# Small matmuls of a linear-attention kernel issued as 32x32 blocks instead of block-diagonal pairs

## The chip, the cores and the metric

The kernel runs on one core of a Trainium2 chip. The core has a matrix engine (PE, with its weight loads shown as PEld), a vector engine (DVE), a scalar engine (ACT), a general-purpose engine (POOL) and a queue engine for transfers (SP), which run in parallel and wait for each other through semaphores (in the kernel before, PE, DVE, ACT and POOL are busy for 244.6, 187.9, 184.3 and 169.9 of 289.8 us, and POOL waits 46.9 us for ACT at line 914). The metric is the device time in microseconds, lower is better; medians of several executions are quoted. Profiled executions show a span, from the first to the last instruction, that is about 1.7 us shorter than the time measured for the same execution. PE's clock is granted at full or at half rate in the clock records of the two traces, which begin at 60.9 us before and 72.5 us after the change. Ahead of that the starts of the matmuls show it: the 128-column transposes of the kernel before (line 643) start 107 ns apart before 60 us and 56 ns apart at 147 to 235 us (medians). "Warm" means the full rate.

## The reference, cut to what matters

```python
# attention: 4 batches, 8 heads, 768 steps, head size 48
k_n = k / (norm(k) + 1e-6)
state = 0                                   # (4, 8, 48, 48)
for t in range(768):
    y[:, :, t] = g[:, :, t] * (q[:, :, t] @ state)
    v_old = state^T k_n[:, :, t]
    state = state + beta[:, :, t] * outer(k_n[:, :, t], v[:, :, t] - v_old)
# then an MLP over 3072 tokens: 384 -> 2048 -> 384
h = x @ w_in
g = where(h >= 1, h, where(h <= -1, 0, (h + 1)**2 / 4))
return g @ w_out
```

The loop over 768 time steps is rewritten in 24 steps of 32. Inside a step the sequential update becomes a 32x32 triangular system for each of 32 pairs of batch and head. The Gram matrix k k^T gives the system, a recursion on 16x16 halves and two merge products invert it, and a masked score matrix k q^T gives the output inside the step.

## The kernel before: the parts that matter

The kernel is a list of tasks. A search in Python decides, before anything runs, the order of the tasks on each engine; then the instructions are emitted in that order. Partitions 0 to 127 hold four batches of 32 rows each. The products below are done for two batches at once, with 64x64 matrices of which only the two diagonal 32x32 blocks are wanted.

```python
# Grams and scores of one step (the unsplit form): 64 rows of stationary, 128 columns moving
for j in range(4 * hf, 4 * hf + 4):
    for G in range(2):                        # two pairs of batches
        r = slice(64 * G, 64 * G + D)
        nc.tensor.matmul(b[64 * G:64 * G + 64, 128 * jj:128 * jj + 128], kt[r, j, 0, :],
                         kt[r, j].rearrange("p a t -> p (a t)"), ...)
# DVE: mask off everything but the lower triangles of the diagonal blocks, twice per step
nc.vector.tensor_tensor(out=amt[:, 4 * hf:4 * hf + 4, 0:128], in0=bank, in1=mask, op=mult)
...
# inverse: DVE transposes 32x32 blocks of the masked Grams, both halves are added, the recursion follows
nc.vector.transpose(out=at, in_=am)           # 128 x 1024
...
# merge products: 32 matrices, block-diagonal stationary
for m in range(32):
    for G in range(2):
        r = slice(64 * G, 64 * G + 64)
        nc.tensor.matmul(b[r, 16 * m:16 * m + 16], am[r, slot + m // J, m % J, 0:64], d0[r, m, 0:16], ...)
...
# masked scores
for j in range(J):
    for G in range(2):
        r = slice(64 * G, 64 * G + 64)
        nc.tensor.matmul(b[r, D * j:D * j + D], amt[r, j, 64:128], u16[r, j, :], ...)
```

Each matmul is two PE instructions in the trace (6,091 LDWEIGHTS and 6,091 MATMUL records in the kernel before): one loads one operand, the stationary matrix, and one streams the other, the moving matrix, through.

Of the kernel before, what the change touches and what calls it, by code (L numbers as in the profile page):

```python
# [33 lines left out]
LAT = 0.12  # L34
# [22 lines left out]
class Task:  # L57
    __slots__ = ("opts", "reads", "writes", "deps", "pred", "succ", "left", "ready", "start", "end", "d", "eng", "fn", "kind", "name", "n",
                 "cost", "nmm", "mode", "gate", "psum", "held", "seq", "lag", "after")
# [35 lines left out]
class Plan:  # L95
# [3 lines left out]
    def add(self, eng, dur, fn, reads=(), writes=(), kind="", name="", alt=(), nmm=0, mode=None, seq=None, prio=0.0):  # L99
        t = Task([(eng, dur, fn)] + list(alt), list(reads), list(writes), kind, name)  # L100
        t.nmm, t.mode, t.n, t.seq = nmm, mode, len(self.tasks), seq
        self.tasks.append(t)
        for v in t.reads:
            v.r.append(t)
        for v in t.writes:
            v.w.append(t)
        return t
# [57 lines left out]
    def forward(self, A):  # L165
        T = self.tasks
        free = dict.fromkeys(ENGS, 0.0)
# [7 lines left out]
        big = []  # L175
# [14 lines left out]
        while left:  # L190
# [48 lines left out]
            if e == "PE":  # L239
                gap = s - free["PE"]  # L240
                if WARM0 < s < WARM1 and gap > 0.6:
                    n = min(int((gap - 0.3) / 0.11 * WSHARE), 24)
                    w = free["PE"] + 0.05
                    warm.append((w, n))
                    big.append((w, w + 0.055 * n))
                    mode = "F"
                while big and big[0][1] < s - 3.4:
                    big.pop(0)
                if sum(y - max(x, s - 3.4) for x, y in big) < 0.8:
                    d *= 1.8  # L250
                if mode is not None and t.mode != mode:
                    d += 0.1
                mode = t.mode
                d = fetch.take(2 * t.nmm, s, d, True)
                if t.mode == "F":
                    big.append((s, s + d))
# [29 lines left out]
            for u in t.succ:  # L286
                u.left -= 1
                r = (t.end if t in u.deps else t.start) + (LAT if e != u.opts[0][0] else 0.0) + u.lag
                if r > u.ready:
                    u.ready = r  # L290
                if not u.left:
                    for o in u.opts:
                        cand[o[0]].append(u)
        self.span = max(t.end for t in T)
        self.warms = warm
        return sorted(order, key=lambda t: (t.start, t.n))

    def backward(self):
# [11 lines left out]
        while n:  # L310
# [14 lines left out]
            for u in t.pred:  # L325
                left[u] -= 1
                r = end + (LAT if e != u.eng else 0.0) + t.lag if u in t.deps else s
# [7 lines left out]
    def plan(self, passes):  # L335
        import random
        rnd = random.Random(7)
        A, best, bestA, stale, hist = self.first(), None, None, 0, []
        for i in range(passes):
            order = self.forward(A)  # L340
            if order is None:
                stale = 9
                hist.append("x")
            else:
                hist.append(round(self.span, 1))
                B = self.backward()
                if best is None or self.span < best[0] - 1e-6:
                    best = (self.span, order, [(t, t.start, t.end, t.eng, [v.bank for v in t.psum]) for t in order], self.warms)
                    bestA, stale = B, 0
                    self.bestA = A  # L350
                else:
                    stale += 1
                A = B
            if stale >= 3:
                A = [x + rnd.gauss(0.0, NOISE) for x in (bestA or A)]
        if PRINT:
            print(hist)
        self.span = best[0]
        for t, t.start, t.end, t.eng, banks in best[2]:
            for v, b in zip(t.psum, banks):  # L360
# [13 lines left out]
def kernel(  # L374
# [42 lines left out]
    mask = tl("mask", [2, 2, 32], FP)  # L417
# [3 lines left out]
    par = tl("par", [2], FP)  # L421
# [14 lines left out]
    AW = 130  # L436
# [3 lines left out]
    R_at = ring("at", 1, [32, 32, 2])  # L440
# [7 lines left out]
    R_p16 = ring("p16", 1, [32, 2, 32])  # L448
# [34 lines left out]
    def load_task(tile_, src, names, cost, val, eng="SP", dur=0.46, kind="load"):  # L483
        def fn(tile_=tile_, src=src):
            ENG[eng].dma_start(out=tile_, in_=src)  # L485
        def fp(tile_=tile_, src=src):
            nc.gpsimd.dma_start(out=tile_, in_=src)  # L487
        t = P.add(eng, dur, fn, [], [val], kind, names, seq="ld",
                  alt=[("POOL", 0.6, fp)] if names[2] in FLEX and int(names[3:]) > 1 else [])
# [51 lines left out]
    vc, vid, vpar = Val("mask"), Val("ident"), Val("par")  # L541
# [6 lines left out]
    def c_mask():  # L548
        nc.gpsimd.memset(ones[:], 1.0)
        nc.gpsimd.memset(mask[:], 0.0)  # L550
        for h4 in range(4):
            r = slice(32 * h4, 32 * h4 + 32)
            nc.gpsimd.affine_select(out=mask[r, :, h4 % 2, :], in_=ones[r, :].rearrange("p (a t) -> p a t", a=2), compare_op=ALU.is_gt, fill=0.0,
                                    base=0, pattern=[[0, 2], [1, 32]], channel_multiplier=-1)

    def c_par():
        nc.gpsimd.memset(par[:], 0.0)
        for h4 in range(4):
            nc.gpsimd.memset(par[32 * h4:32 * h4 + 32, h4 % 2:h4 % 2 + 1], 1.0)
# [5 lines left out]
    P.add("POOL", 1.0, c_ident, [], [vid], "", "ident")  # L565
    P.add("POOL", 1.5, c_mask, [], [vc], "", "mask")
# [8 lines left out]
    P.add("POOL", 0.5, c_par, [], [vpar], "", "par")  # L575
    vtab = Val("tab")
    P.add("DVE", 0.08, lambda: nc.vector.memset(tab[:], 1.0), [], [vtab], "", "tab0")
    P.add("ACT", 1.4, lambda: act("ACT", tab[:], tab[:], AF.Sqrt), [vtab], [Val("tab2")], "", "tab")
# [3 lines left out]
    P.add("POOL", 1.2, lambda: nc.gpsimd.memset(R_p16.tiles[0][:], 0.0), [], [vzp], "", "zp16", alt=[("DVE", 0.91, lambda: nc.vector.memset(R_p16.tiles[0][:], 0.0))])  # L582
# [4 lines left out]
    def prep_pair(p):  # L587
# [5 lines left out]
        P.add("ACT", acost(768), lambda: act("ACT", sqt[:], flat(kt_), AF.Square), [kv], [sq], "", f"ksq{p}",  # L593
# [6 lines left out]
        P.add("DVE", 0.2, lambda: nc.vector.reciprocal(out=nt[:, 3], in_=nt[:, 2]), [v2, nv], [v3], "", f"rcp{p}")  # L600
# [54 lines left out]
    def gram(s):  # L655
        gi = s // GS
        kv, kt = vkt[s]
        vq = vqt[s]
        av, amt = R_am.new(f"am{s}")
        mv = R_mm.new(f"mm{s}")[0]  # L660
        vam[s] = (av, amt, [mv])
        if SPLIT[gi]:
            for v_, a_ in ((av, 0), (mv, 1)):
                gp = pv("c", f"gp{s}_{a_}")

                def fn(gp=gp, a_=a_):
                    b = bk(gp)
                    for j in range(J):
                        for G in range(2):
                            r = slice(64 * G, 64 * G + D)  # L670
                            nc.tensor.matmul(b[64 * G:64 * G + 64, 64 * j:64 * j + 64], kt[r, j, 0, :], kt[r, j, a_, :], start=(j == 0), stop=True, skip_group_check=True)  # L671
                P.add("PE", pe_dur(16, 20), fn, [kv] + (vq if a_ else []), [gp], "fill", f"{'gh'[a_]}r{s}", nmm=16, mode="Q", seq="hr" if a_ else "gr")
                if a_ == 0 and gi < NSPLIT:
                    for sl in range(2):
                        P.add("ACT", acost(256), lambda gp=gp, sl=sl: act("ACT", amt[:, :, 32 * sl:32 * sl + 32], _ap(bk(gp), [[64, J], [1, 32]], 32 * sl), scale=par[:, sl:sl + 1]),
                              [gp, vpar], [v_], "", f"m{s}_{a_}")
                    continue
                P.add("DVE", dcost(512), lambda gp=gp, a_=a_: nc.vector.tensor_tensor(  # L678
                    out=amt[:, :, 64 * a_:64 * a_ + 64], in0=bk(gp)[:].rearrange("p (j x) -> p j x", j=J),
                    in1=_ap(mask, [[0, J], [1, 64]], 64 * a_), op=ALU.mult), [gp, vc], [v_], "", f"m{s}_{a_}")  # L680
            return
        for hf in range(2):
            gp = pv("c", f"gp{s}_{hf}")

            def fn(gp=gp, hf=hf):
                b = bk(gp)
                for j in range(4 * hf, 4 * hf + 4):
                    for G in range(2):
                        r = slice(64 * G, 64 * G + D)
                        jj = j - 4 * hf  # L690
                        nc.tensor.matmul(b[64 * G:64 * G + 64, 128 * jj:128 * jj + 128], kt[r, j, 0, :], kt[r, j].rearrange("p a t -> p (a t)"),
                                         start=(jj == 0), stop=True, skip_group_check=True)
            P.add("PE", pe_dur(8, NS_GR), fn, [kv] + vq, [gp], "fill", f"gr{s}_{hf}", nmm=8, mode="Q", seq="gr")
            P.add("DVE", dcost(512), lambda gp=gp, hf=hf: nc.vector.tensor_tensor(
                out=amt[:, 4 * hf:4 * hf + 4, 0:128], in0=bk(gp)[:].rearrange("p (j x) -> p j x", j=4),
                in1=_ap(mask, [[0, 4], [1, 128]]), op=ALU.mult), [gp, vc], [av, mv], "", f"m{s}_{hf}")

    def inverse(gi):
# [4 lines left out]
        def op(n, kind, reads, writes, name, **aps):  # L703
            def make(e):
                return (e, dcost(n) if e == "DVE" else pcost(n) + (0.12 if name[0] == "s" else 0.0),
# [4 lines left out]
        P.add("DVE", dcost(1024), lambda: nc.vector.transpose(out=at[:].bitcast(FP).rearrange("p a t w -> p (a t w)"), in_=_wap(am, [[1, 32], [AW // 2, 32]], slot * J * AW // 2)),  # L710
              avs, [tv], "", f"at{gi}")
        xv, x = R_x.new()
        for blk in range(2):
            o = 8 * blk * 64 + 32 * blk
            op(256, ALU.add, [tv], [xv], f"prea{gi}", out=_ap(x, [[32, 8], [16, 2], [1, 16]], 256 * blk),
# [334 lines left out]
```

## Time and profile before

| | before |
|---|---|
| time, median (lowest to highest) | 291.06 us (289.87 to 291.66), 3 runs |
| PE instructions (weights and matmuls) | 12,184 |
| first state product (line 834) / first MLP matmul (line 906) | 42.9 / 54.3 us |
| last PE matmul starts | 282.7 us |
| busy: PE, DVE, ACT, POOL | 244.6, 187.9, 184.3, 169.9 us of 289.8 |

The page and the timeline of this profile are read in the prediction below, with its lines. The timeline gives start, duration, engine, source line, operation and, in brackets, the idle time before it with what ended it. "x14" means fourteen such instructions in a row, and "issue" means that the engine waited for nothing that the profile shows.

### The profile page before, as it was taken

To read this page: it belongs to the slowest core of one execution; us is meant where nothing else is said; L and a number is where in the kernel's file an instruction comes from. 1 tells how busy PE (TensorE), PEld (TensorE's weight loads), DVE (VectorE), ACT (ScalarE), POOL (GpSimd) and SP (SyncE) were. 2 spreads that over 40 slices of the span, in tenths; PEclk is the share of its full clock that TensorE was granted. 3 is DMA by queue.
4 is the path that set the end of the run, shared out by engine and by line. 5 is a ranking of instruction groups with operands and counts; after the bars stand their busy time and mean duration, and the time that the engine had idled before them with its cause. 6 is when DMAs were issued, how large, how long until landed. Compare 5 with 4: busy or idle time off the path is not lost.

```text
span 289.8 us, 13941 instructions
## 1 busy us (share of the span) xinstructions
PE 244.6 (84%) x6091; PEld 161.6 (56%) x6091; DVE 187.9 (65%) x348; ACT 184.3 (64%) x325; POOL 169.9 (59%) x309
## 2 busy tenths in 40 slices
PE   0266497895979989996799999999999999999990
PEld 0254486674856665653556565665657555555560
DVE  3699996864875546895687787767954375456200
ACT  1664344377456878965888587887683686797410
POOL 7693059592768794798873598841882272354000
PEclk9999999999587999999699999999999999999997
DMA  6689575989398575277421267532421110111121
GB/s 107 106 173 167 91 141 92 219 129 184 50 208 149 101 123 136 56 152 161 101 41 43 60 128 154 105 81 50 88 56 33 32 32 3 31 32 33 49 79 53
DMA packets 88525, 27.74 MB, mean 96 GB/s; under 512 B 80320, under 2 KB 86976, under 8 KB 88464
## 3 DMA queue, kind: packets, MB, share of 16 engines
q1 hardware_dynamic: 77456, 18.35, 32.7%
q0 software_dynamic: 6752, 7.72, 14.3%
q10 hardware_dynamic: 4256, 0.79, 1.5%
q8 instruction: 47, 0.77, 1.1%
q14 instruction: 14, 0.11, 0.1%
HBM read 25.26 MB, written 4.72 MB: 103 GB/s over the span
## 4 chain that ended last, share of the span: by engine, by line
PE 60%; DVE 13%; DMA 8%; issue 6%; POOL 5%; ACT 3%; SPq 3%; ACTq 0%; DVEq 0%; POOLq 0%
PE bank L933 19%; PE bank L906 18%; DMA rk<-in_k_dram 6%; POOL rk L487 3%; DVE xx L706 3%; PE bank L769 3%; SPq L485 3%; PE bank L671 2%; PE sps L846 2%; PE bank L860 2%; PE bank L834 2%; PE bank L643 2%; DVE tm L706 2%; DMA rv<-in_v_dram 2%; PE bank L876 2%
## 5 line engine op out<-in xcount | busy, mean ns | idle before, releaser
L906 PE MATMUL bank<-xt,win 128*128 128x512 f16 (+1 forms) x336 | 79.1, 369 | 2.2 <-issue 1.4
L917 DVE SCALAR_TENSOR_TENSOR gt<-bank,r 128x512 f16<-128x512 f32 x96 | 64.1, 682 | 24.2 <-ACT r L471 12.7
L933 PE MATMUL bank<-wout,gt 128*128 128x384 f16 x384 | 72.6, 327 | 0.0
L471 ACT ACTIVATE rl<-bank 128x512 f32<-128x512 f32 x96 | 56.4, 597 | 17.3 <-PE bank L906 15.4
L914 POOL TENSOR_TENSOR r<-rl 128x512 f16<-128x512 f32 x26 | 26.8, 1039 | 49.2 <-ACT rl L471 46.9
L933 PEld LDWEIGHTS <-gt 128*128 128x128 f16 x384 | 34.9, 98 | 23.6
L906 PEld LDWEIGHTS <-win 128*128 128x128 f16 x336 | 31.0, 102 | 24.2 <-issue 3.2
L471 ACT ACTIVATE r<-rl 128x512 f16<-128x512 f32 x70 | 43.2, 628 | 0.9
L487 POOL DMA_DIRECT2D rk<-in_k_dram x38 | 22.0, 584 | 6.0 <-DMA win<-in_moe_w_in_dram 3.6
L471 ACT ACTIVATE s<-sps 128x768 f16<-128x768 f32 x23 | 18.6, 810 | 9.1 <-PE sps L846 8.6
L706 POOL TENSOR_TENSOR xx<-xx,tm 128x100 f32<-128x100 f32 (+6 forms) x57 | 19.8, 347 | 6.8 <-DVE tm L706 2.5
L471 ACT ACTIVATE ot<-bank 128x384 f32<-128x384 f32 x24 | 11.8, 490 | 18.6 <-PE bank L933 18.6
L614 PE MATMUL bank<-ident,kn 64*64 64x64 f16 x384 | 9.9, 212 | 15.3 <-DVE kn L605 11.9
L706 POOL TENSOR_TENSOR tm<-xx 128x108 f32<-128x108 f32 (+6 forms) x59 | 19.8, 335 | 4.9 <-DVE xx L706 0.5
L864 DVE TENSOR_TENSOR y<-bank,rg 128x384 f16<-128x384 f32 x24 | 13.2, 551 | 13.4 <-PE bank L860 13.3
L471 ACT ACTIVATE u<-bank 128x384 f16<-128x384 f32 x24 | 11.7, 487 | 16.0 <-PE bank L834 14.6
L678 DVE TENSOR_TENSOR am<-bank,mask 128x512 f16<-128x512 f32 x24 | 16.1, 685 | 5.6 <-PE bank L671 5.3
L603 POOL TENSOR_TENSOR kn<-rk,nn 128x768 f16<-128x768 f32 x10 | 14.7, 1475 | 8.5 <-DVE nn L600 7.4
L471 ACT ACTIVATE kt<-bank 128x1024 f16<-128x1024 f16 x14 | 14.2, 1024 | 7.6 <-PE bank L614 6.7
L614 PEld LDWEIGHTS <-kn 64*64 64x64 f16 x384 | 8.6, 127 | 17.3 <-DVE kn L605 12.0
L595 DVE TENSOR_REDUCE nn<-ksq 128x16 f32<-128x768 f32 x12 | 11.3, 942 | 10.4 <-ACT ksq L471 10.4
L671 PE MATMUL bank<-kt 48*64 48x64 f16 x512 | 14.7, 217 | 2.5 <-DVE kt L621 1.6
(88 smaller groups left out, 395.7 us busy)
## 6 DMA issues: line engine op xcount, KB each, us to landing
out_dram<-ot SPq DMA_DIRECT2D x24, 192.0 KB
rq<-in_q_dram SPq DMA_DIRECT2D x22, 192.0 KB
rg<-in_g_dram SPq DMA_DIRECT2D x72, 48.0 KB
rv<-in_v_dram SPq DMA_DIRECT2D x67, 48.0 KB
rk<-in_k_dram SPq DMA_DIRECT2D x50, 48.0 KB
rk<-in_k_dram POOLq DMA_DIRECT2D x38, 48.0 KB, 3.1
win<-in_moe_w_in_dram POOLq DMA_DIRECT2D x4, 384.0 KB, 7.8
wout<-in_moe_w_out_dram POOLq DMA_DIRECT2D x4, 384.0 KB, 6.7
```

Of the source, the lines that this page charges most:

```text
L471: nc.scalar.activation(out=out, in_=in_, func=func, **kw)
L487: nc.gpsimd.dma_start(out=tile_, in_=src)
L603: P.add("POOL", 1.5, lambda: nc.gpsimd.tensor_tensor(out=knf, in0=flat(kt_), in1=_ap(nt, [[1, 2 * J], [0, D]], 3 * 2 * J), op=ALU.mult), [ ...
L614: nc.tensor.transpose(b[r, cj * 64:cj * 64 + 64], at_[r, cj * D:cj * D + 64], ident[r, 64 * G:64 * G + 64])
L671: nc.tensor.matmul(b[64 * G:64 * G + 64, 64 * j:64 * j + 64], kt[r, j, 0, :], kt[r, j, a_, :], start=(j == 0), stop=True, skip_group_check ...
L678: P.add("DVE", dcost(512), lambda gp=gp, a_=a_: nc.vector.tensor_tensor(out=amt[:, :, 64 * a_:64 * a_ + 64], in0=bk(gp)[:].rearrange("p (j ...
L706: lambda: ENG[e].tensor_tensor(op=kind, **aps))
L864: P.add("DVE", dcost(384), lambda: nc.vector.tensor_tensor(out=y16[:], in0=_ap(bk(yp), [[D, J], [1, D]]), in1=gt_[:, c], op=ALU.mult), [yp ...
L906: nc.tensor.matmul(b[:, x * nt:x * nt + nt], win[:, kt_, m * 128:m * 128 + 128], xt[:, kt_ * nt:kt_ * nt + nt], start=(kt_ == 0), stop=(kt ...
L914: P.add("POOL", pcost(512), lambda: nc.gpsimd.tensor_tensor(out=r2[:], in0=rl[:], in1=rl[:], op=ALU.mult), [rv], [r2v], "elem", f"r2{u}_{i ...
L917: P.add("DVE", dcost(512), lambda: nc.vector.scalar_tensor_tensor(out=gt[:], in0=bk(hp)[:], scalar=1.0, in1=r2[:], op0=ALU.max, op1=ALU.mi ...
L933: nc.tensor.matmul(b[:, 0:DM], gt[:, o:o + 128], wout[:, m, :], start=(m == 0), stop=(m == NM - 1))
```

## The change

The intent is to compute only what is wanted: each 32x32 block is a matmul of its own, four of them side by side, so Grams and scores fill half the columns, and masks and transposes on DVE halve. The core of the diff:

```diff
-    mask = tl("mask", [2, 2, 32], FP)
+    mask = tl("mask", [2, 32], FP)
-    AW = 130
+    AW = 66
...
-    for G in range(2):
-        r = slice(64 * G, 64 * G + D)
-        nc.tensor.matmul(b[64 * G:64 * G + 64, 128 * jj:128 * jj + 128], kt[r, j, 0, :], kt[r, j]..., )
+    for h4 in range(4):
+        r = slice(64 * (h4 // 2), 64 * (h4 // 2) + D)
+        t_ = slice(32 * (h4 % 2), 32 * (h4 % 2) + 32)
+        nc.tensor.matmul(b[32 * h4:32 * h4 + 32, ...32 * n columns], kt[r, j, 0, t_], kt[r, j, a0:a0 + n, t_], )
...
-    for G in range(2):
-        r = slice(64 * G, 64 * G + 64)
-        nc.tensor.matmul(b[r, 16 * m:16 * m + 16], am[r, slot + m // J, m % J, 0:64], d0[r, m, 0:16], )
+    for h4 in range(4):
+        r = slice(32 * h4, 32 * h4 + 32)
+        nc.tensor.matmul(b[r, 16 * m:16 * m + 16], am[r, slot + m // J, m % J, 0:32], d0[r, m, 0:16], )
... (second merge product and masked scores likewise; the additions of the two halves before the recursion go)
-UNITS = [2, 2, 4, 4, 4, 4, 4]
+UNITS = [2, 2, 4, 4, 4, 4, 2, 2]
-LIMITS = {'c': 4, 'm': 3, 'o': 1}
+LIMITS = {'c': 5, 'm': 3, 'o': 1}
-WARM0, WARM1, WSHARE = 16.0, 60.0, 0.6          # dummy matmuls between 16 and 60 us
+WARM1 = 0.0                                     # none
-PASSES = 60
+SEEDS = [198018091]
```

It also rewrites the search (a model of the PE clock, one seed instead of 60 noisy passes), reorders the loads and lets POOL issue more of them. The order of nearly every instruction differs.

## The prediction

> **What bounds the kernel now.** I read the page's busy row first, then the strip of forty slices, then busy time per ten microseconds, then the timeline of the matrix engine.
>
> ```profile
> PE 244.6 (84%) x6091; PEld 161.6 (56%) x6091; DVE 187.9 (65%) x348; ACT 184.3 (64%) x325; POOL 169.9 (59%) x309
> ...
> PE   0266497895979989996799999999999999999990
> ...
> q8 instruction: 47, 0.77, 1.1%
> ```
>
> The matrix engine (PE) leads, DVE and ACT are a fifth lower, and PE is full only in the right half. So there are two regimes. Up to about 54 us, where the first MLP matmul runs, a chain of latencies decides: loads, norms, the recursive inverse of the first group on DVE, two merge products, then the first state steps. After that the order of PE's work decides.
>
> The time after 54 us can be counted. From start to start, warm, the trace gives 216 ns for an MLP-in matmul of 512 columns, 163 ns for an MLP-out one, about 17 ns for a 64x64 product (two side by side), 7 to 9 ns for a 32-column block product (four side by side). Multiplying by the counts, what PE still has to do after 54.3 us is 185 us; it takes until 282.8, that is 228 us. So about 43 us are lost after the start. The timeline shows where:
>
> ```profile
> 69.14 0.27 PE L834 MATMUL bank<-rr,zz 32*32 32x48 f16 x14
> 72.01 0.38 PE L834 MATMUL bank<-rr,zz 32*32 32x48 f16 x18 [2.61 <-issue]
> ...
> 84.28 0.26 PE L815 MATMUL bank<-s,kt 48*32 48x48 f16 x9
> 86.49 0.33 PE L815 MATMUL bank<-s,kt 48*32 48x48 f16 x23 [1.95 <-issue]
> ```
>
> A run of 32 matmuls of one task, with all operands present, breaks in the middle and "issue" is named. There are six such breaks over half a microsecond after 54 us (55.2, 65.1, 69.2, 84.4, 101.9, 161.8), 9.2 us in all, and every one lies at matmul 94 plus a multiple of 128. One matmul is two instructions (weights, matmul), so that is every 256 instructions, and 12,184 PE instructions make 47.6 such blocks: the 47 transfers of the instruction queue, each 16,384 bytes in the trace. Their starts are never closer than 3.5 us, and the next block never begins less than 1.3 us after its transfer has landed. [...]
>
> The other losses are loads and a cold clock:
>
> ```profile
> 70.00:80.00 10.00, 7.63 (x245) 6.87 (x244) 7.52 (x14) 4.71 (x8) 5.96 (x9) 0.56 0.47 70
> ...
> 126.47 1.64 POOL rk L487 x3
> 128.10 0.07 issue
> 128.18 2.30 POOL rk L487 x4
> 130.47 5.94 DMA rk<-in_k_dram
> ```
>
> In the first line the column before the DMA share is PE's clock: 0.56. It is halved at 71.1 to 81.4, 88.2 to 91.6 and 139.4 to 146.2, each time after PE had stood still. The other lines (the chain of waits) show a k load holding everything from 126 to 136 us. Between 70 and 90 and 130 and 150 PE does 21 us of warm work in 40: 19 of the 43 lost microseconds (two of the breaks, 4.9 us at most, are in them).
>
> [...]
>
> **The change, part by part.** It also rewrites the schedule search (clock and fetch in its model, one seed) and load order, so no instruction stays in its place.
>
> PE work. Grams: 512 matmuls of 64x64 at 20 ns and 128 of 64x128 at 33 ns (14.4 us) become 1024 blocks at 8 ns (8.2): minus 6.2. Merges: 768 at 16.6 ns (12.8) become 1536 at 7 ns (10.8): minus 2. Masked scores: 384 at 18 ns (6.9) become 768 at 8 ns (6.1): minus 0.8. Dummies: 51 at 56 ns, minus 2.9. Total 201.6 to about 190 us, warm.
>
> PE instructions. 1536 more attention matmuls, 48 more since the last MLP unit is halved, 51 fewer dummies: 7624 pairs, 15,250 instructions in the new order, 59.6 blocks. Twelve more blocks at 3.5 us or above is the price.
>
> DVE. Masking falls from 40 to 20 operations of 0.68 us (minus 13.7); the transpose before the inverse halves, 6 of 2.01 us to 6 of about 1.05, as the 512-wide one at the end takes (minus 5.7). ACT: 16 masks of 0.47 become 4 of 0.6 (minus 5.1), 12 merge copies of 0.69 become 6 of 0.6 (minus 4.6), one table load of 1.28 fewer. POOL: the pre-additions go, minus about 6. None of these engines is the bound after 54 us; it shortens chains.
>
> Startup. In the old timeline of DVE, the transpose of group 0 starts at 19.35 and the first state product runs at 42.94. Out of that chain go 0.95 (transpose), about 0.8 (the two additions 1.13, with 0.69 for one scaling becoming about 1.1 for two), 0.6 (second ACT copy), and about 2 because group 1's transpose (1.93) no longer stands between the two output transposes. I put the first state product 4 to 5 us earlier, near 38. But the new order puts 1640 instructions, 6.4 blocks, between it and the first MLP matmul, which now follows both merge products of group 1. At 3.6 to 4.5 us a block (loads are heaviest there) that is 23 to 29 us: first MLP at about 63, later than before, with 173.5 us of warm work left. The old kernel at 63 has about 180 left. Net gain at that point: 6 to 7 us.
>
> After it. I cut each order into blocks of 256 instructions, took the warm work of each and raised it to 3.6 us where lower. Before: 185 + 15 = 200 us. After: 173.5 + 30 = 203.6. Of the 15 only 9.2 appeared as breaks, the rest fell in waits that existed anyway. If the same 0.6 holds, 18 of the 30 appear: PE needs 173.5 + 18 = 191.5, against 185 + 9 = 194. So the saved work is nearly eaten by fetch.
>
> That leaves the waits. Before, 43 minus 9 = 34 us went to loads, cold clock and chain waits. Now last units of two steps instead of four let attention run later beside MLP work, a fifth PSUM bank is allowed to attention, any SP load may go to POOL, and the search counts cold windows. I guess 21 of the 34 stay. Sum: 63 + 191.5 + 21 + 7 (PE's end at 282.8 to the end at 289.8: last copy and store) = 282; with cold windows wholly avoided some 6 less. I take 280.
>
> **Rivals.** One: fetch becomes the bound everywhere. All 30 us of shortfall appear and loads stretch the fetch beyond 3.6; then 63 + 203.6 + 21 + 7 = 295, slower. For it: blocks at 0.9 to 2 us of warm work stand in rows early on. Against: stalls and other waits overlap, and the search models them. Two: the loads decide. Waits near 85 to 91 and 126 to 136 come from buffer-limited loads on SP and POOL, which the change hardly touches; then the 34 us remain, and 63 + 191.5 + 34 + 7 = 295, no gain. For it: the data loaded is the same; against: the order was searched anew. Three: the search removes nearly all cold and idle time after the start, 10 left of 34: 63 + 191.5 + 10 + 7 = 271.
>
> **Range and chances.** 271 and 295 are ends, 280 between; since a rewritten search with better terms more likely removes waits than adds them, I put 270 to 292. Under 285.2 is faster by 2%: 0.66. Within 2%: 0.28. Slower: 0.06.
>
> **What would show it.** Right: about 59 instruction transfers, more breaks after 54 us at distances of 128 matmuls, 15 us or more in all; DVE busy near 167, ACT near 173; first state product near 38 and first MLP near 63; fewer half-clock windows. Wrong: breaks no longer than before (then the time falls to about 271 or lower), or gaps before state products named after k, v, g loads as long as before (then no gain).

The sum came to 63 + 191.5 + 21 + 7 = 282.5 us, and 280 was taken. The times for one product, the 3.6 to 4.5 us a block and the 21 us of waits in it are my estimates. The old trace shows 16.2 ns from start to start of the 64x64 products of line 671 (mean, warm) and 6.4 ns for the 32-column products of lines 805 and 834 (9.6 before 60 us); between 54 and 78 us the instruction transfers start 3.6 to 6.0 us apart, and at 50 to 60 us all transfers move 202 GB/s, the most of any ten microseconds. PE's idle times at or before the three half-clock stretches last 2.6, 1.95 and 2.6 us (until 72.0, 86.5 and 138.8).

## The result, and the profile after

The changed kernel takes 308.31 us (median of 4, 307.02 to 310.11) against 291.36 us for the kernel before in the same rounds. The ratio is 1.060 (95% interval 1.052 to 1.067): six per cent slower, far outside the predicted 270 to 292. A ratio in this text is the mean time of one kernel's fast runs over that of the other's in the same rounds, so it is not quite the ratio of the medians.

The page of the changed kernel, its busy row, its PE strip and the instruction queue:

```profile
PE 231.3 (76%) x7624; PEld 152.1 (50%) x7624; DVE 170.7 (56%) x318; ACT 175.0 (57%) x306; POOL 185.7 (61%) x334
...
PE   0263154635879898797897969999987999899991
...
q8 instruction: 59, 0.97, 1.3%
```

Every engine but POOL is busy for less time, as intended, and the kernel is slower. The instruction queue moved 59 blocks instead of 47. The timeline of PE shows what that costs:

```profile
62.79 0.31 PE L781 MATMUL bank<-zz,p 32*32 32x16 f16 x21 [2.73 <-issue]
...
65.22 0.34 PE L691 MATMUL bank<-kt 48*32 48x64 f16 x11
68.99 0.47 PE L691 MATMUL bank<-kt 48*32 48x64 f16 x21 [3.43 <-issue]
...
71.02 1.74 PE L918 MATMUL bank<-xt,win 128*128 128x256 f16 x8
76.01 1.01 PE L918 MATMUL bank<-xt,win 128*128 128x256 f16 x4 [3.25 <-issue]
```

These are the breaks of the prediction, longer and one after another. The start of every matmul and of every instruction transfer can be read from the trace; here are four consecutive blocks of 128 matmuls of the changed kernel, worked out from those starts (us):

```
block begins   transfer for the next block    next block begins   block took   after landing
58.79          60.41 to 61.28                 62.79               4.00         1.51
62.79          66.76 to 67.71                 68.99               6.20         1.28
68.99          73.50 to 74.43                 76.01               7.02         1.58
76.01          78.22 to 79.43                 80.83               4.83         1.40
```

In these four the transfer for the next block starts only after the present block has begun and takes about 1 us, and the next block begins 1.3 to 1.6 us after it has landed. I call a gap at a block boundary a break when it exceeds the usual distance of the matmul before it by 0.15 us or more and ends 1.1 to 1.75 us after the landing of a transfer. The kernel before has 6 breaks of 9.2 us in all; the changed one has 24 of 37.0 us, 14.8 of them before the first MLP matmul. The longest distance from start to start at a break is 2.8 us before and 3.7 us after.

The other difference is the start. The first transpose before an inverse (line 710 before, 727 after) shows it, first in the kernel before, then in the changed one, each with the work of ACT that precedes it (ACTq is ACT's queue issuing loads):

```profile
9.62 0.22 ACT L471 ACTIVATE nn<-nn 128x16 f32<-128x16 f32 x1
9.74 0.83 ACT L471 ACTIVATE ksq<-rk 128x768 f32<-128x768 f32 x1
...
19.35 2.01 DVE L710 STREAM_TRANSPOSE at<-am 128x1024 f32<-128x1024 f32 x1
```

```profile
6.03 5.81 ACTq L513 DMA_DIRECT2D rk<-in_k_dram  x4
11.88 0.21 ACT L499 ACTIVATE nn<-nn 128x16 f32<-128x16 f32 x1 [7.62 <-DMA rk<-in_k_dram]
12.01 1.56 ACT L499 ACTIVATE qn<-rq 128x768 f16<-128x768 f32 x2
15.22 0.84 ACT L499 ACTIVATE ksq<-rk 128x768 f32<-128x768 f32 x1 [1.66 <-DMA rk<-in_k_dram]
...
22.95 1.09 DVE L727 STREAM_TRANSPOSE at<-am 128x512 f32<-128x512 f32 x1
```

The transpose itself takes half as long, as planned, but starts 3.6 us later. ACT is issuing k loads until 11.84, takes the first root at 11.88 (9.62 before), then converts q, and squares the second block of k at 15.22 (9.74 before). The first state product is at 44.2 us (42.9 before), the first MLP matmul at 71.0 (54.3 before).

### The profile page after: what moved, and what is told of

Read it like the earlier page. It is cut to its first block, busy times and chain, and to the rows that moved or that the text cites. A ratio compares the mean times of both kernels' runs of the same rounds, so it can differ in the third digit from the quotient of the medians.

```text
span 305.6 us, 16979 instructions
## 1 busy us (share of the span) xinstructions
PE 231.3 (76%) x7624; PEld 152.1 (50%) x7624; DVE 170.7 (56%) x318; ACT 175.0 (57%) x306; POOL 185.7 (61%) x334
## 4 chain that ended last, share of the span: by engine, by line
PE 48%; POOL 16%; issue 14%; DVE 9%; DMA 6%; ACT 3%; SPq 2%; POOLq 0%; DVEq 0%; ACTq 0%
PE bank L945 16%; PE bank L918 15%; POOL xx L723 6%; POOL tm L723 4%; DVE xx L723 2%; DMA rq<-in_q_dram 2%; PE sps L858 2%; SPq L513 2%; DMA rg<-in_beta_dram 2%; PE bank L817 2%; PE bank L846 2%; PE bank L872 2%; DMA rg<-in_g_dram 2%; PE bank L781 2%; PE bank L769 2%
## 5 line engine op out<-in xcount | busy, mean ns | idle before, releaser
L929 DVE SCALAR_TENSOR_TENSOR gt<-bank,r 128x512 f16<-128x512 f32 x96 | 63.1, 682 | 32.2 <-ACT r L499 16.3
L945 PE MATMUL bank<-wout,gt 128*128 128x384 f16 x384 | 75.2, 332 | 1.9 <-issue 1.9
L926 POOL TENSOR_TENSOR r<-rl 128x512 f16<-128x512 f32 x30 | 30.9, 1039 | 62.6 <-ACT rl L499 60.4
L918 PEld LDWEIGHTS <-win 128*128 128x128 f16 x384 | 35.4, 100 | 28.1 <-issue 9.7
L499 ACT ACTIVATE r<-rl 128x512 f16<-128x512 f32 x66 | 40.7, 628 | 1.6
L515 POOL DMA_DIRECT2D rk<-in_k_dram x45 | 26.2, 588 | 8.2 <-DMA win<-in_moe_w_in_dram 3.0
L723 POOL TENSOR_TENSOR tm<-xx 128x100 f32<-128x100 f32 (+6 forms) x59 | 19.8, 335 | 6.9 <-DVE xx L723 2.7
L635 PE MATMUL bank<-ident,kn 64*64 64x64 f16 x384 | 10.6, 216 | 17.3 <-DVE kn L626 14.6
L515 POOL DMA_DIRECT2D rg<-in_g_dram x36 | 21.2, 593 | 1.6 <-issue 0.8
L624 POOL TENSOR_TENSOR kn<-rk,nn 128x768 f16<-128x768 f32 x10 | 14.8, 1477 | 11.9 <-DVE nn L621 7.8
L834 DVE TENSOR_TENSOR rr<-rv,bank 128x384 f16<-128x384 f32 x23 | 12.7, 552 | 13.5 <-PE bank L817 10.3
L691 PE MATMUL bank<-kt 48*32 48x32 f16 (+1 forms) x1024 | 13.0, 193 | 9.4 <-issue 5.2
```

What stands on the lines that cost most here:

```text
L499: nc.scalar.activation(out=out, in_=in_, func=func, **kw)
L515: nc.gpsimd.dma_start(out=tile_, in_=src)
L624: P.add("POOL", 1.5, lambda: nc.gpsimd.tensor_tensor(out=knf, in0=flat(kt_), in1=_ap(nt, [[1, 2 * J], [0, D]], 3 * 2 * J), op=ALU.mult), [ ...
L635: nc.tensor.transpose(b[r, cj * 64:cj * 64 + 64], at_[r, cj * D:cj * D + 64], ident[r, 64 * G:64 * G + 64])
L691: nc.tensor.matmul(b[32 * h4:32 * h4 + 32, o + 32 * n * j:o + 32 * n * j + 32 * n], kt[r, j, 0, t_], kt[r, j, a0:a0 + n, t_], start=(o == ...
L723: lambda: ENG[e].tensor_tensor(op=kind, **aps))
```

## The experiments

Fourteen kernels were run. A frozen order means that the search was left as it was and only what the tasks emit was altered, so the order of the tasks on every engine stays the same.

### 1 and 2: take the extra instructions out of the changed kernel

The same order, but two batches in one matmul again. The shapes in PSUM (the memory that PE writes to) are kept, so the other engines have the same work in the same order. The sums are wrong.

```diff
-    for h4 in range(4):
-        nc.tensor.matmul(b[32 * h4:32 * h4 + 32, ...], kt[r, j, 0, t_], kt[r, j, a0:a0 + n, t_], )
+    for G in range(2):
+        nc.tensor.matmul(b[64 * G:64 * G + 64, ...], kt[r, j, 0, :], kt[r, j, a0:a0 + n, 0:32], )
... (merges and masked scores likewise, with 64-column stationary matrices)
```

> The changed kernel in its own order, every other engine's instructions unchanged, but grams, merges and masked scores issued as pairs of 64-row matmuls again: half as many of them, same data shapes in PSUM, wrong results on purpose. PE instructions 15,250 -> 11,922. Fetch theory (the 16 KB instruction blocks arrive too slowly): the breaks at 128-matmul distances, 37 us in the changed kernel, fall under 12 us and the time falls from 308 to 278-288. Rival (the poorer schedule and load order cost the time): within 2% of 308.

In the second run only the merge products are changed back:

> As the run before, but only the merge products are pairs again (768 fewer matmuls, 1536 fewer PE instructions, six blocks of 256; wrong results on purpose). Fetch theory: between, the breaks fall from 37 to about 24-28 us, the time to 294-301. Rival schedule theory: within 2% of 308.

Measured: 291.55 us (ratio to before 1.004, 0.999 to 1.009) with 2 breaks of 2.2 us, and 299.88 us (1.033, 1.024 to 1.041) with 14 breaks of 21.3 us. The full undoing ends 3.5 us above the expected range, the half lies in it; the breaks are as expected in the first run and under the expected 24 to 28 us in the second. Of the first run, PE's timeline where the changed kernel stood still:

```profile
63.49 0.63 PE L691 MATMUL bank<-kt 48*64 48x64 f16 x16 [1.34 <-ACT kt L499]
64.08 0.50 PE L888 MATMUL bank<-ident,y 128*128 128x128 f16 x3
64.51 0.63 PE L691 MATMUL bank<-kt 48*64 48x64 f16 x16
65.08 0.51 PE L817 MATMUL bank<-s,kt 48*32 48x48 f16 x32
65.40 0.51 PE L827 MATMUL bank<-s,kt 48*32 48x48 f16 x32
65.84 2.74 PE L918 MATMUL bank<-xt,win 128*128 128x256 f16 x12
```

In this stretch no group is broken in the middle, and the only wait has an engine's name. The twelve MLP matmuls that took from 71.02 to 77.0 us in the changed kernel are through in 2.74. What follows: the extra PE instructions account for 16.8 us, nearly all of the 17 us that the change lost, and the rival (a poor order) does not explain that part. It also follows that without them the change gains nothing: 291.6 us against 290.5, with less work on PE and 17 us less on DVE.

### 3 and 4: put the extra instructions into the kernel before

The reverse: the kernel before in its own order and with its own data, right results, but its block-diagonal matrices are used a block at a time.

```diff
-    for G in range(2):
-        r = slice(64 * G, 64 * G + 64)
-        nc.tensor.matmul(b[r, 16 * m:16 * m + 16], am[r, slot + m // J, m % J, 0:64], d0[r, m, 0:16], )
+    for h4 in range(4):
+        r = slice(32 * h4, 32 * h4 + 32)
+        nc.tensor.matmul(b[r, 16 * m:16 * m + 16], am[r, slot + m // J, m % J, 32 * (h4 % 2):32 * (h4 % 2) + 32], d0[r, m, 0:16], )
... (second merge, Grams and masked scores likewise)
```

> The kernel before in its own order, all other engines unchanged, but its grams, merges and masked scores issued as 32-column blocks, right results: 12,184 -> 15,768 PE instructions, about 5 us less warm PE work. Fetch theory: breaks rise from 9 to 30 us or more and the time from 291 to 303-315. Rival (schedule, loads): the same or a little faster, 286-292.

> As the run before, but only the merge products are blocks (1536 more PE instructions, six fetch blocks). Fetch theory: breaks 14-20 us, time 295-302. Rival: 290-292.

Measured: 322.87 us (1.113, 1.106 to 1.119) with 26 breaks of 37.3 us; merges alone 308.54 us (1.059, 1.051 to 1.067; its profiled execution took 304.7) with 17 breaks of 23.2 us. Both are slower than expected by the fetch theory and opposite to the rival. The page and the timeline of the first of them:

```profile
PE   0374546659768989897898779998797999999991
...
q8 instruction: 61, 1.00, 1.3%
```

```profile
40.41 0.71 PE L671 MATMUL bank<-kt 48*32 48x64 f16 x38
43.74 1.41 PE L671 MATMUL bank<-kt 48*32 48x64 f16 x90 [2.62 <-issue]
...
56.95 0.30 PE L671 MATMUL bank<-kt 48*32 48x64 f16 x8
59.13 0.63 PE L671 MATMUL bank<-kt 48*32 48x64 f16 x56 [1.89 <-issue]
```

Only the cutting of PE's products was changed here, with about 5 us less warm PE work (an estimate by the prediction's times for one product), and the kernel is 32 us slower. The runs in one table:

| kernel | PE instructions | breaks, us | time, us |
|---|---|---|---|
| changed, all pairs | 11,922 | 2.2 | 291.6 |
| changed, merges as pairs | 13,714 | 21.3 | 299.9 |
| changed | 15,250 | 37.0 | 308.3 |
| before | 12,184 | 9.2 | 290.5 |
| before, merges as blocks | 13,720 | 23.2 | 308.5 |
| before, all blocks | 15,768 | 37.3 | 322.9 |

Six blocks of instructions of the merges cost 8.4 us in one order and 18 in the other; the breaks grow by 14 to 16 us in both. So the order decides what a break costs: in the changed kernel half of it is hidden by other waits; in the kernel before the time grows by more than the breaks do, and where the rest comes from was not traced.

### 5: the old search on the changed body

```diff
-    order = P.plan(SEEDS)
+    order = P.plan(PASSES)      # the earlier search, 60 noisy passes, and its dummies
```

> The changed kernel's body, units and load order, but the schedule found by the old search (60 noisy passes, dummies between 16 and 60 us). It issues at least as many PE instructions (15,250 and dummies). Fetch theory: breaks stay near 30-40 us and the time 303-313. Rival (the new search found a bad order): under 298.

Measured: 310.09 us (1.070, 1.063 to 1.078) with 30 breaks of 37.8 us. Another order of the same 15,000 instructions breaks for as long and takes as long. The new search is not what made the kernel slow.

### 6: fewer bytes on the transfer engines at the start

The blocks of 6.2 and 7.0 us stand where weights are loaded. In the trace, the delay from the start of a block to the start of the transfer for the next one, over the first 3 us of a block, has a median of about 1.0 us where other transfers keep the 16 transfer engines under 0.2 busy on average and 2.0 us (at most 4.5; 12 blocks) where they keep them over 0.9 busy; in the kernel before 0.7 and 2.3 (6 blocks). To try it, the weights were loaded at an eighth of their bytes and the rest filled with constants on DVE and ACT before the first k arrives. Its output is wrong, which doesn't matter for the time.

```diff
-    src = ...ap=[[DFF, 128], [128 * DFF, 3], [1, 512]])
+    src = ...ap=[[DFF, 128], [128 * DFF, 3], [1, 64]])
```

> The changed kernel in its own order, weights loaded at an eighth of their bytes (the rest filled by two constants early on idle engines; wrong on purpose). If instruction blocks queue behind loads: blocks that took 6.2 and 7.0 us near 63 to 76 take under 4.5, breaks before 80 us fall from about 22 to 10-15 us, time 297-303. If the block time is fixed: breaks before 80 us 20 us or more, time 306-310.

Measured: 307.26 us (1.064, 1.059 to 1.069), breaks 28.6 us in all, 16.3 of them up to the boundary at 81.39 us against 19.0 up to the same boundary (80.83) in the changed kernel: above the 10 to 15 expected. The two long blocks took 4.00 and 4.55 us instead of 6.20 and 7.02, about as expected if they queue behind loads. The time is a miss, and the experiment is flawed: the constants delayed the start, the first state product came at 49.4 instead of 44.2. What is measured is that blocks were shorter with lighter loads and that the transfer for the next block starts later with busy transfer engines (2.0 us against 1.0); that it queues behind the loads is my reading and was not shown, and the run doesn't price it.

### 7 and 8: is the saved DVE time worth anything?

In the changed order, each DVE mask and each transpose before an inverse is issued twice, so DVE gets back what the change saves:

```diff
-    lambda gp=gp, ...: nc.vector.tensor_tensor(out=amt[:, :, 0:64], ...)
+    lambda gp=gp, ...: [nc.vector.tensor_tensor(out=amt[:, :, 0:64], ...) for _ in range(2)]
```

> The changed kernel in its own order with each mask on DVE and each transpose before an inverse issued twice, so DVE gets back the 20 us that the halved data saved. If DVE's saving lies off the path: within 3 us of 308. If it was worth what it saves: 318 or more.

Measured: 314.1 and 315.6 us in the two fast executions (two more, 319.3 and 321.6, are slow; ratio 1.089, 1.082 to 1.095), DVE busy 190.5 instead of 170.7: 6 to 9 us for 20 us of work, between the two expectations. The reverse, on the kernel before, cuts DVE by about 10 us (13 were planned) from the third group on. Its output is wrong, which doesn't matter for the time.

```diff
+    w = 8 if gi > 1 and a_ else 64       # of the second mask only an eighth
-    transpose(out=at, in_=am[... 32 ...])
+    transpose(out=at[:, 0:h], in_=am[... h ...])   # h = 16 from the third group on
```

> The kernel before in its own order, but from the third group of steps on every second mask on DVE is cut to an eighth of its columns and the transpose before the inverse is halved (wrong on purpose), so DVE does about 13 us less, as in the changed kernel; PE's instructions stay. If the saved DVE time is on the path: 4 to 9 us faster than before. If it is hidden: within 1.5 us of before.

Measured: 289.68 us (0.997, 0.992 to 1.003), DVE busy 177.4 instead of 187.9. So in the later groups, in the order that was tuned for it, DVE's time was hidden. The first two groups, whose inverses lie in the start, were left out of this test.

### 9 to 14: the start

Only q0's loads were put behind k1's:

```diff
+    q0 = [t for t in order if t.name == "ldq0"]      # emitted after the last load of k1
```

> The changed kernel in its own order, only q0's four loads issued behind k1's on each queue. If q0 in front of k1 delays the first inverse: first state product 1.5 to 4 us earlier than 44.2 and the time 1 to 4 us shorter than 308. If instruction fetch sets the pace from there on: the start is earlier but the first MLP matmul stays near 71 and the time within 1 us.

Measured: 310.96 us (1.071, 1.066 to 1.077), the first state product at 45.3: a miss for both. It does not settle whether q0 makes the start late: ACT's order still has two conversions of q ahead of the second k, and ACT now waits 1.92 and 1.00 us for q's loads there.

With the breaks gone (experiment 1) the first MLP matmul is at 65.8, still 11.5 us later than before. The chain of waits of that run shows POOL's load issues between steps of the second group's inverse, so I moved those loads to SP, without and with the block matmuls:

```diff
+    if t.kind == "load" and t.eng == "POOL" and t.opts[0][0] == "SP" and 37.0 < t.start < 53.0:
+        t.fn = t.opts[0][2]              # issue on SP
```

> The changed kernel with pairs as in e1_after_pairs (wrong on purpose), and the g, k and v loads that POOL issues between 37 and 53 us of the plan issued by SP instead, so that POOL's part of group 1's inverse is not held up by them. If POOL's issuing delays the first MLP matmul (65.8 us in e1_after_pairs): first MLP at 61 to 64 and the time 2 to 5 us under 291.5. If the k load itself sets it: within 1 us.

> The changed kernel with the same loads moved from POOL to SP and its block matmuls kept. If instruction fetch sets the pace of the start, the first MLP stays within 1.5 us of 71 and the time within 1.5 us of 308 although POOL is freed; if POOL sets it, 3 to 5 us faster.

Measured: 302.17 us (1.044, 1.036 to 1.051) with the first MLP matmul at 80.8, and 316.11 us in the fast executions (a fourth, 322.57, is slow; ratio 1.090, 1.075 to 1.105) with it at 78.8. Both are worse than the kernels that they were made from, by 10.6 and some 8 us, so both expectations failed. But the edit made a longer delay of its own. PE's line in the first of them, which stands ahead of the first MLP matmul:

```profile
78.44 0.64 PE L691 MATMUL bank<-kt 48*64 48x64 f16 x16 [14.62 <-ACT kt L499]
```

SP issues the moved loads one after another, from 51.1 to 66.2 us on the chain of waits, and ACT can square the k of that Gram only at 75.4, after a load that landed at 75.3. So whether POOL's issuing delays the start is not shown. What experiment 1 does show is which wait ends last there: the order puts a Gram of a later group ahead of the first MLP matmul, and that Gram needs a k load that POOL issued at 55.1 to 56.0 and that landed at 60.3. What the start would be with another order stays open.

In the kernel before, ACT loads two activation tables (1.28 us each, at 6.17 and 8.32 us), the second between the first square and the first square root. Loading the square root's table right after the first four loads should leave one, as in the changed kernel, whose trace has one table load, at 2.77 us:

```diff
+    early = [t for t in order if t.name in ("tab0", "tab")]     # emitted behind the first four k loads
```

> The kernel before in its own order, only the activation table of the square root is loaded right after the first four k loads are issued (one table load instead of two). If the first norm waits for the tables: 1 to 2.5 us faster than before, 288-290. If k's transfer or DVE sets the start: within 0.5 us.

Measured: 287.87 us against 289.3 (0.995, 0.992 to 0.999), first state product at 40.9 instead of 42.9. It is the fastest kernel, by half a per cent. Without the dummies as well:

> The kernel before in its own order with the activation table loaded first and without the dummies: 286.5 to 289 if both edits are harmless, that is at least 1.5 us faster than before; 289 or more if the dummies were needed.

Measured: 292.04 us (1.003, 0.999 to 1.008). The two ratios differ by 0.8%, so the dummies seem to be worth about that; the two runs were made in different rounds. Alone, without the table:

> The kernel before in its own order without its 51 dummy matmuls, which the change also drops (12,082 PE instructions). If the dummies hold the clock up: PE turns warm later than 60.9 us and the time rises by 1 to 3 us. If they do nothing but fill gaps: within 1 us of before, 289 to 292.

Measured: 292.13 us in the three fast executions (1.003, 0.996 to 1.010), which decides nothing.

## Why the prediction was wrong, point by point

**The mechanism was right, and the price and the gain were wrong.** Blocks of 256 instructions that arrive too slowly were seen in the old trace (six breaks, 9.2 us); twelve more of them were counted, and 59 transfers came. The first rival, "fetch becomes the bound everywhere", made 295 us and is nearest to what happened, but not by its terms: 22.2 of its 30 us of shortfall appeared. In one sum: 71.0 + 173.5 + 22.2 + 32.1 (waits) + 6.8 (tail) = 305.6, the profiled span, where the prediction had 63 + 173.5 + 18 + 21 + 7 = 282.5. The 23 us between them are 8 at the start, 4 of breaks and 11 of waits.

**The step that failed most is "I guess 21 of the 34 stay".** PE's time from 71.0 to 298.8 us is 227.8. Less 173.5 of warm work and 22.2 of breaks that leaves 32.1 us of other waits: hardly any of the 34 went. Nor did they go where the breaks were gone: in experiment 1 the same sum is 217.1 - 176.5 - 2.2, some 38 us (the 176.5 is an estimate by the prediction's times for one product). The second rival, "the loads decide", foretold the number, but its reason is not what the traces show. On the chain of waits after the first MLP matmul the loads and their issuing took 30.8 us before and 17.7 in the changed kernel, while POOL's steps of the inverse took 0.7 and 32.9. Which waits cost PE its 32 us stays open.

**The start was put 8 us too early, because of its first half.** The first state product was put near 38 and came at 44.2. The chain from the first transpose to it did shrink, from 23.6 to 21.3 us, by 2.3 instead of 4 to 5, but that transpose starts 3.6 us later. A break of 1.75 us fell into the second merge product; without it, in experiment 1, the state product came no earlier (44.6). From there to the first MLP matmul the 23 to 29 us foretold were right: 26.8.

**"If the same 0.6 holds, 18 of the 30 appear" was low.** The 30 are counted after the first MLP matmul, where the breaks measure 22.2 us, 0.74 of them. The 0.6 came from six breaks of one order. To raise every block with less warm work to 3.6 us is too simple: in the old trace the block from 167.65 to 170.64 took 2.98 us and no break ended it, and in the changed kernel the blocks that a break ended took from 2.75 to 7.02. In the four blocks shown, a block's time is the delay to the start of the transfer, about 1 us of transfer, and 1.3 to 1.6 us after the landing; it is the delay that varies (1.62 to 4.51 us).

**These terms are not independent.** Taking the extra instructions away shortened the span by 16.0 us (305.6 to 289.6): 5.2 before the first MLP matmul and 10.7 after it, where 20 us of breaks went but other waits grew by about 6 (38 against 32.1).

**What was right.** The warm work after the first MLP matmul (173.5, a count), DVE at 170.7 (near 167 foretold) and ACT at 175.0 (173). POOL was foretold at 6 us less and has 16 us more. The 6 us went, but POOL issues 118 loads of k, v and g instead of 91, at 0.59 us each, and does four more of the MLP's operations (4.2 us): this cost of the new load order and schedule was not in the sum. The merge products, put at 7 ns a block, start 8.2 ns apart (median, warm) where the pairs start 15.9 ns apart, so the 2 us foretold for them were not there. Half-clock stretches after the first MLP matmul took 17.1 us in the changed kernel's profiled execution and 20.5 before, hardly fewer, and two of its other three executions had a lower mean clock (0.865 and 0.877 against 0.965).

**Where the gain went.** By the prediction's times the change saved about 9 us of PE work besides the dummies (about 7 without the merges), and DVE is busy for 17 us less. Twelve instruction blocks cost 16.8 us in the changed order. Without them (experiment 1) the first MLP matmul still comes 11.5 us later than before, but with some 8.5 us less work left for PE (176.5 against 185); after it the waits are no shorter, and the time is that of the kernel before.

## What to carry to other kernels

Count the instructions, not only the work: where matmuls are small, divide PE's order into the blocks that the instruction transfers show (here 47 transfers of 16,384 bytes for 12,184 PE instructions and 59 for 15,250, one for every 256) and look for short blocks in a row. Here transfers started 3.3 us apart at the closest in the changed kernel, and a block that a break ended took up to 7.02 us, while all transfers moved 200 GB/s. A group of matmuls that breaks in its middle with "issue" as the reason was the sign of it, and cutting matmuls into parallel smaller ones made this kernel slower although every engine but POOL was busy for less time. A saving of 10 us on DVE, which other waits hid, was worth nothing in the old order (289.7 against 290.6 us), and the new order brought costs of its own.
